# A fused attention and maxout kernel: the key and value projection of five batches moves into a down-layer bank at the first group spot

## The chip, the cores and the metric

The kernel runs on one core of a Trainium2 chip, as one program with one launch. The metric is the device time of one execution in microseconds (us). TensorE (PE) multiplies matrices and writes to PSUM; VectorE (DVE) and ScalarE (ACT) copy, add and evaluate functions; GpSimd (POOL) and SyncE (SP) issue the transfers here. Each engine works through its own instructions in the order in which the program gives them.

## The reference: what is computed

```
k_proj = einsum('ks,bhsd->bhkd', E, k);  v_proj = einsum('ks,bhsd->bhkd', F, v)
attn   = softmax(q @ k_proj^T / sqrt(64))          # over 64 projected keys
x      = (attn @ v_proj), heads side by side        # 8192 tokens x 512
out    = maximum(x @ w1, x @ w2) @ w_out            # 512 -> 1024 -> 512
```

There are 8 batches with 8 heads, 1024 positions and head size 64. Inputs and output are float32; the kernel multiplies in fp16.

## The kernel before

**Up and down layer.** With wd = w1 - w2 and m = w2 @ w_out, the output is relu(x @ wd) @ w_out + x @ m. From the second half-batch on, both matrix products are done as 2x2 block products with 7 block multiplications in place of 8. This needs sums of blocks of x (`sums_x`), of the relu'd activations (`sums_g`) and of the weights, all on VectorE (line 519).

**Units.** The 16 units are (batch, half of the positions), n = 0 to 15. While unit n does its down layer, unit n+1's up layer runs between. The down layer of a unit has 7 products (p1, p2, p6, p5, p7, p3, p4, line 636), each cut in three pieces of 4 matmuls in units 1 to 14. I write Pa.b for piece b of the a-th of them, from P0.0 to P6.2. The up layer of a unit has 14 products of 4 matmuls (line 558): seven, U0 to U6, after each of two group spots G0 and G1. A group spot does one step of attention for a later batch: the scores of a new group of heads (line 266), and the row sums and attention values of the group before (line 278).

**The order** is written out by hand in a list of slots; `at_slot` hangs steps behind a slot. For odd and even units n > 1 it is, with h = 0 first:

```
P0.0 P0.1 G0 P0.2 P1.0 | U0 P1.1 U1 P1.2 U2 P2.0 U3 P2.1 U4 P2.2 U5 P3.0 U6
P3.1 P3.2 G1 P4.0 P4.1 P4.2 | U0 P5.0 U1 P5.1 U2 ... U5 P6.2 U6
```

Unit 1 has three pieces ahead of G0 and three behind, and in its second half two ahead of G1 and one behind.

**PSUM.** There are four banks mm0 to mm3 and two pairs of banks "att". The down layer owns mm0 and mm1: products p1, p6, p7 and p4 build up in one (X), p2, p5 and p3 in the other (Y); X is mm0 in even units and mm1 in odd ones. The up layer and the scores use mm2 and mm3, sums and values the att pairs.

**What empties the banks.** ACT: the exponentials of the scores (line 355, two per spot), the logarithm of the sums (374), its inversion (377), copies of up and down products that are used twice (529), the last down product (704). DVE: the additions of the up layer (573, relu in 576), of the down layer (660), and the scaling of the attention values (381). In the up layer U0 and U2 build up in one bank, so U2 waits for the copy (529) of U0.

**Projection of k and v** (`step_kv`, line 180): 16 matmuls, 8 pairs of k and v side by side, for one batch. For batches 3 to 7 it hangs behind U1 of the first half of unit n = 2b-3 (units 3, 5, 7, 9, 11), in an att bank. Behind it come an ACT copy of k (line 191), and, one slot later, on DVE a copy of v (196), a second copy of k (198) and of v (200); then SP issues the transposing transfer of k (223), POOL waits for its landing (229) and issues the loads of the next batch (102). At G0 of the same unit SP has issued two transposing transfers of q (249). The new batch's first scores come at G1 of that unit. Batch 2 has its projection in unit 1, also in an att bank and behind U1, and this stays.

**Block sums for unit 2.** For the up layer of unit 2, which runs in unit 1, the sum S(2) = X(0,0) - X(1,0) hangs behind P1.2 of unit 1, and it is what U4 multiplies:

```
elif n == 2:
    where = (("P", 1, 0, 2), 0), (("P", 1, 1, 0), 1), (("P", 1, 1, 2), 2), (("U", 1, 0, 1), 3)
```

Later units have their sums behind slots of the second half of unit n-2. Steps behind a slot stand in the order in which they were hung there; behind P1.2 these are the addition of P1 (line 660), one sum of g and then S(2).

**The last unit** (15) has no up layer beside it; its seven products run in one piece each, and the last (p4) is emptied in two halves (line 699).

Of the kernel before, what the change touches and what calls it, by code (L numbers as in the profile page):

```python
# [16 lines left out]
def kernel(  # L17
# [42 lines left out]
    def mm_bank(dtype=FP32, n=None):  # L60
        if n is None:
            n = turn.pop(0)
            turn.append(n)
        return ps.tile([128, 512 if dtype == FP32 else 1024], dtype, tag=f"mm{n}", name="mm_ps")

    def att_banks(dtype=FP32):
        return ps.tile(
            [128, 2, 512 if dtype == FP32 else 1024], dtype, tag="att", bufs=2, name="att_ps"
        )
# [99 lines left out]
        t["qt"] = qtp.tile([128, H, HALF], FP16, tag="qt", name="qt_sb")  # L169


    def step_kv(t, h0=0, h1=H, which="kv", att=False, dma=False):
        kv_ps = att_banks()[:, 0, :] if att else mm_bank()
        n = (h1 - h0) * D
        both = which == "v"
        for c in range(NC):
            for w in which:
                i = "kv".index(w)
                for r in range(2) if both else (i,):
                    nc.tensor.matmul(  # L180
                        out=kv_ps[r * KP : (r + 1) * KP, 0:n],
                        lhsT=eft[:, i, c, :],
                        rhs=t[w][:, h0:h1, c, :],
                        start=(c == 0), stop=(c == NC - 1),
                    )
        fl = lambda ap: ap[:, h0:h1].rearrange("p h z d -> p (h z d)")
        zd = lambda ap: ap.rearrange("p (h d z) -> p h z d", d=D // 2, z=2)
        if "k" in which:
            eng = nc.vector.tensor_copy if which == "k" else nc.scalar.copy
            kp = t["kp"][:, h0:h1]  # L190
            eng(out=kp[:, :, 0, :], in_=kv_ps[0:KP, 0:n].rearrange("p (h d) -> p h d", d=D))
        if both:
            nc.vector.tensor_copy(out=t["vp"][:, h0:h1], in_=zd(kv_ps[:, 0:n]))
        elif "v" in which:
            def finish_v():
                nc.vector.tensor_copy(out=t["vp"][KP:128, h0:h1], in_=zd(kv_ps[KP:128, 0:n]))
                if dma:
                    nc.vector.tensor_copy(out=kp[:, :, 1, :], in_=kp[:, :, 0, :])
                    step_kpt_dma(t)
                nc.vector.tensor_copy(out=fl(t["vp"][0:KP]), in_=fl(t["vp"][KP:128]))  # L200

            if att:
                return finish_v
            finish_v()
# [405 lines left out]
    def down_steps(u, alone):  # L610
        b, o = u["b"], u["o"]
        st = {}
        xbank, ybank = (0, 1) if u["n"] % 2 == 0 else (1, 0)

        def cat(g, x):
            return lambda n: g[:, n] if n < NG else x[:, n - NG]

        def product(k, name, n, lo=0, hi=2 * (NG + NX)):
            if n is not None and (lo == 0 or alone):
                st[name] = mm_bank(n=n)  # L620
            bank = st[name]
            A = lambda j, h: cat(g_blk(u, j, h), x_blk(u, j, h))
            S = lambda i: cat(s_g(i), s_x(i, u))
            Bb = lambda h, c: cat(
                wo_sb[:, h * NG : (h + 1) * NG, c * CH : (c + 1) * CH],
                m_sb[:, h * NX : (h + 1) * NX, c * CH : (c + 1) * CH],
            )
            T = lambda i: lambda n: T_sb[:, i, n, :]
            a, w_ = {
                1: lambda: (A(0, 0), Bb(0, 0)), 2: lambda: (A(0, 1), Bb(1, 0)),  # L630
                3: lambda: (S(3), Bb(1, 1)), 4: lambda: (A(1, 1), T(3)),
                5: lambda: (S(0), T(0)), 6: lambda: (S(1), T(1)), 7: lambda: (S(2), T(2)),
            }[k]()
            for m in range(lo, hi):
                i, c = divmod(m, NG + NX)
                nc.tensor.matmul(  # L636
                    out=bank[:, i * CH : (i + 1) * CH],
                    lhsT=a(c)[:, i * 128 : (i + 1) * 128],
                    rhs=w_(c),
                    start=(n is not None and m == (lo if alone else 0)),  # L640
                    stop=(c == NG + NX - 1), skip_group_check=True,
                )
            return bank

        two = lambda ap: ap.rearrange("q (i m) -> q i m", i=2)

        def o_tile():
            return opool.tile([128, 2, CH], FP32, tag="o", name="o_sb")

        def store(j, c, o_sb, i0=0, i1=2):  # L650
            nc.sync.dma_start(
                out=out.rearrange("(n p i o) m -> n o p i m", p=128, i=NI, o=2)[
                    b, j, :, 2 * o + i0 : 2 * o + i1, c * CH : (c + 1) * CH
                ],
                in_=o_sb[:, i0:i1],
            )

        def add(j, c, x, y):
            o_sb = o_tile()
            nc.vector.tensor_tensor(out=o_sb, in0=two(x), in1=two(y), op=ALU.add)  # L660
            store(j, c, o_sb)

        def keep_d(bank):
            return keep("pd", bank, *([nc.vector.tensor_copy] if u["n"] == 0 else []))

        size = 2 * (NG + NX) // (1 if alone else 2 if u["n"] == 0 else 3)

        def piece(k, name, n, m):
            product(k, name, n, m, m + size)

        def whole(k, name, n):
            return product(k, name, n, 2 * (NG + NX) - size)

        def p1():
            st["s1"] = keep_d(whole(1, "X", xbank))

        def p2():
            add(0, 0, whole(2, "Y", ybank), st["s1"])

        def p6():  # L680
            st["u1"] = keep_d(whole(6, "X", None))

        def p5():
            st["s5"] = keep_d(whole(5, "Z", ybank))

        def p7():
            st["u2"] = keep_d(whole(7, "X", None))

        def p3():
            add(0, 1, whole(3, "Z", None), st["u1"])  # L690
            add(1, 1, st["u2"], st["s5"])

        def p4():
            o_sb = o_tile()
            if alone:
                for i in range(2):
                    bank = product(4, ("C", i), 2 + i, 6 * i, 6 * i + 6)
                    part = slice(i * CH, (i + 1) * CH)
                    nc.vector.tensor_tensor(
                        out=o_sb[:, i], in0=bank[:, part], in1=st["u2"][:, part], op=ALU.add,  # L700
                    )
                    store(1, 0, o_sb, i, i + 1)
                return
            nc.scalar.copy(out=o_sb, in_=two(whole(4, "X", None)))
            store(1, 0, o_sb)

        steps_ = (
            (p1, 1, "X", xbank), (p2, 2, "Y", ybank), (p6, 6, "X", None), (p5, 5, "Z", ybank),
            (p7, 7, "X", None), (p3, 3, "Z", None), (p4, 4, "X", None),
        )  # L710
        return [
            (*(lambda a=a, m=m: piece(*a, m) for m in range(0, 2 * (NG + NX) - size, size)), f)
            for f, *a in steps_
        ]
# [67 lines left out]
    for n, key in enumerate(units):  # L782
        downs = down_steps(U[key], n == last)
        if n in (0, last):
            for p, pieces in enumerate(downs):
                slots += [(("P", n, p, i), x) for i, x in enumerate(pieces)]
            continue
        pieces = [(("P", n, p, i), x) for p, x in enumerate(downs) for i, x in enumerate(x)]
        ups = [*up_steps(U[units[n + 1]])]
        for h, (x, y) in enumerate(((3, 3), (2, 1)) if n == 1 else ((2, 2), (2, 3))):  # L790
            slots += pieces[:x]
            slots.append((("G", n, h), lambda: None))
            slots += pieces[x : x + y]
            del pieces[: x + y]
            for i in range(7):
                slots.append((("U", n, h, i), ups.pop(0)))
                if i < 6:
                    slots.append(pieces.pop(0))
        assert not pieces and not ups
# [52 lines left out]
    for b in range(3, B):  # L852
        t = tiles[b]
        n = 2 * b - 3
        at_slot(("G", n, 0), new_attn, t)
        at_slot(("G", n, 0), step_qt_dma, t, 0, H // 2)
        at_slot(("G", n, 0), step_qt_dma, t, H // 2, H)
        at_slot(("U", n, 0, 1), step_kv, t, 0, H, "kv", True, True)
        at_slot(("U", n, 0, 6), step_gate, t)
        at_slot(("U", n, 0, 6), loads, b + 1, "k", "v", "q")  # L860
    groups = [(tiles[b], g, j) for b in range(1, B) for j in range(2) for g in range(2)][2:]
# [67 lines left out]
```

## Time and profile before

| | |
|---|---|
| five runs, median (lowest, highest) | 329.0 us (328.65, 330.51) |
| the profiled execution, its own time | 328.65 us |
| its span from first to last instruction | 326.9 us |
| copies at line 529 | 172, 593 ns each, 97.2 us |
| exponentials at line 355 | 50, 597 ns each |
| scaling at line 381 | 26, 1219 ns each |
| additions at line 660 (one input in PSUM) | 32, 685 ns each |
| output stores | 63 of 256 KB, 2.7 us to landing, and 2 of 128 KB |
| loads of v, of q | 17.3 and 22.0 us to landing |

The profile gives, for each engine, when an instruction started and how long it took, and in brackets how long the engine had been idle and what released it. Matmuls overlap: the modelled duration of one 128x256 matmul is 273 ns, but four of them in a row start 0.437 us before the next four. So on PE one reads the starts, and a delay is a distance between starts that is longer than it should be. The rows of the timeline merge neighbours of one kind ("x4").

### The profile page before, as it was taken

How to read it: one execution, taken by the hardware profiler on the slowest of the kernel's cores; microseconds unless marked ns; L12 is line 12 of the kernel's file. 1: busy time of each engine (PE TensorE's matmuls, PEld its weight loads, DVE VectorE, ACT ScalarE, POOL GpSimd, SP SyncE). 2: the span in 40 equal slices, each digit the busy share in tenths (PEclk: the TensorE clock that was granted, in tenths of full speed). 3: DMA queues.
4: the chain of work that ended last, by engine and by line, in shares of the span. 5: the costliest groups of instructions: out<-in, count | busy, mean ns of one | idle time of the engine just before them, and what ended most of it. 6: DMA issues, size and time to landing. Idle time of an engine off the chain costs nothing.

```text
span 326.9 us, 9015 instructions
## 1 busy us (share of the span) xinstructions
PE 317.4 (97%) x3856; PEld 248.6 (76%) x3856; DVE 239.5 (73%) x424; ACT 201.2 (62%) x359; POOL 36.9 (11%) x56
## 2 busy tenths in 40 slices
PE   8979999999999999999999999999999999999994
PEld 3544446877888788878887888878887888888883
DVE  1346798985969878677967796877967796969572
ACT  2465232666777577677776777657776777765541
POOL 8646002003000110003000300003000000000000
PEclk9999999999999999999999999999999999999999
DMA  8999999988999899996999599888999130212032
GB/s 157 205 198 176 207 207 208 218 189 156 184 239 232 125 154 237 195 194 96 213 221 183 109 183 244 194 162 122 226 191 213 43 99 32 98 34 98 33 130 96
DMA packets 74680, 53.14 MB, mean 163 GB/s; under 512 B 29456, under 2 KB 74512, under 8 KB 74640
## 3 DMA queue, kind: packets, MB, share of 16 engines
q0 software_dynamic: 29376, 28.31, 54.8%
q1 hardware_dynamic: 45264, 24.25, 31.0%
q8 instruction: 30, 0.49, 0.6%
q14 instruction: 10, 0.08, 0.1%
HBM read 57.15 MB, written 16.78 MB: 226 GB/s over the span
## 4 chain that ended last, share of the span: by engine, by line
PE 79%; DMA 14%; POOL 2%; DVE 2%; issue 1%; ACT 0%; DVEq 0%; POOLq 0%
PE mm_ps L636 43%; PE mm_ps L558 26%; DMA q_sb<-in_q_dram 8%; DMA v_sb<-in_v_dram 4%; PE att_ps L180 3%; PE att_ps L278 3%; PE mm_ps L266 3%; DMA big<-in_moe_w_dram 2%; POOL q_sb L102 1%; POOL k_sb L102 1%; DVE gt_sb L573 1%; PE mm_ps L237 1%; DVE o_sb L660 1%; POOL v_sb L102 0%; DVE xt_sb L381 0%
## 5 line engine op out<-in xcount | busy, mean ns | idle before, releaser
L529 ACT COPY p_sb<-mm_ps 128x512 f32<-128x512 f32 x172 | 97.2, 593 | 42.9 <-PE mm_ps L558 30.6
L636 PEld LDWEIGHTS <-big 128*128 128x128 f16 x768 | 73.6, 98 | 12.0 <-issue 3.5
L636 PE MATMUL mm_ps<-T_sb,big 128*128 128x256 f16 x576 | 77.9, 273 | 0.0
L573 DVE TENSOR_TENSOR gt_sb<-mm_ps,p_sb 128x512 f16<-128x512 f32 x56 | 38.5, 688 | 45.8 <-PE mm_ps L558 42.6
L558 PE MATMUL mm_ps<-big,big 128*128 128x256 f16 x336 | 50.4, 273 | 0.0
L558 PEld LDWEIGHTS <-big 128*128 128x128 f16 x448 | 43.8, 98 | 5.3 <-issue 0.2
L636 PEld LDWEIGHTS <-gt_sb 128*128 128x128 f16 x384 | 35.7, 98 | 9.7 <-issue 5.4
L636 PE MATMUL mm_ps<-wo_sb,gt_sb 128*128 128x256 f16 x256 | 42.9, 273 | 0.1
L558 PEld LDWEIGHTS <-wd_sb 128*128 128x128 f16 x336 | 32.9, 98 | 4.1 <-issue 0.4
L558 PE MATMUL mm_ps<-xt_sb,wd_sb 128*128 128x256 f16 x224 | 33.6, 273 | 0.2 <-ACT ex_sb L355 0.2
L355 ACT ACTIVATE ex_sb<-mm_ps 128x512 f16<-128x512 f32 x50 | 27.2, 597 | 9.6 <-PE att_ps L278 7.0
L381 DVE TENSOR_TENSOR xt_sb<-att_ps,ld_sb 128x1024 f16<-128x1024 f32 x26 | 31.7, 1219 | 0.1
L660 DVE TENSOR_TENSOR o_sb<-mm_ps,p_sb 128x512 f32<-128x512 f32 x32 | 21.9, 685 | 11.0 <-PE mm_ps L636 7.5
L636 PE MATMUL mm_ps<-m_sb,xt_sb 128*128 128x256 f16 x128 | 24.4, 273 | 0.0
L608 ACT ACTIVATE gt_sb<-mm_ps 128x512 f16<-128x512 f32 x28 | 16.8, 600 | 8.7 <-PE mm_ps L558 8.7
L519 DVE TENSOR_TENSOR big<-gt_sb 128x1024 f16<-128x1024 f16 x32 | 21.9, 684 | 0.2
L576 DVE TENSOR_SCALAR gt_sb<-gt_sb 128x512 f16<-128x512 f16 (+1 forms) x56 | 20.3, 363 | 1.9
L636 PE MATMUL mm_ps<-T_sb,gt_sb 128*128 128x256 f16 x128 | 21.5, 273 | 0.0
L636 PE MATMUL mm_ps<-wo_sb,big 128*128 128x256 f16 x128 | 21.5, 273 | 0.0
L636 PEld LDWEIGHTS <-xt_sb 128*128 128x128 f16 x192 | 18.8, 98 | 2.2
L229 POOL COPY junk<-kpt_sb 1x1 f16<-1x1 f16 x5 | 0.9, 178 | 162.1 <-DMA kpt_sb<-kp_sb 162.1
L573 DVE TENSOR_TENSOR gt_sb<-p_sb 128x512 f16<-128x512 f32 x28 | 19.1, 682 | 0.0
(85 smaller groups left out, 428.1 us busy)
## 6 DMA issues: line engine op xcount, KB each, us to landing
out_dram<-o_sb SPq DMA_DIRECT2D x63, 256.0 KB, 2.7
k_sb<-in_k_dram POOLq DMA_DIRECT2D x7, 1024.0 KB, 10.0
v_sb<-in_v_dram POOLq DMA_DIRECT2D x7, 1024.0 KB, 17.3
q_sb<-in_q_dram POOLq DMA_DIRECT2D x7, 1024.0 KB, 22.0
k_sb<-in_k_dram POOLq DMA_DIRECT2D x4, 256.0 KB, 6.4
q_sb<-in_q_dram POOLq DMA_DIRECT2D x4, 256.0 KB, 7.5
v_sb<-in_v_dram POOLq DMA_DIRECT2D x2, 512.0 KB, 12.5
big<-in_moe_w_dram POOLq DMA_DIRECT2D x8, 128.0 KB, 10.9
```

The costliest lines, as they stand in the source:

```text
L180: nc.tensor.matmul(out=kv_ps[r * KP : (r + 1) * KP, 0:n], lhsT=eft[:, i, c, :], rhs=t[w][:, h0:h1, c, :], start=(c == 0), stop=(c == NC - 1),)
L266: nc.tensor.matmul(out=banks[e][pos : pos + Z, h * W : (h + 1) * W], lhsT=t["kpt"][o * D : (o + 1) * D, head, s * Z : (s + 1) * Z], rhs=t[ ...
L355: nc.scalar.activation(out=t["ex", g, j][:, e, :], in_=banks[e], func=ACTF.Exp, scale=scale)
L381: nc.vector.tensor_tensor(out=x_out(t, g, j).rearrange("q z o n -> q o z n"), in0=at_ps.rearrange("q o (z n) -> q o z n", z=2), in1=ld[:, ...
L519: nc.vector.tensor_tensor(out=S(i), in0=x, in1=y, op=op)
L529: copy(out=x, in_=bank)
L558: nc.tensor.matmul(out=bank[:, m * W : (m + 1) * W], lhsT=w_[:, n_, (2 * d + m) * 128 : (2 * d + m + 1) * 128], rhs=a[:, n_, :], start=(n ...
L573: nc.vector.tensor_tensor(out=c_blk(j, c), in0=two(x), in1=two(y), op=ALU.add)
L576: nc.vector.tensor_scalar_max(ap, ap, 0.0)
L608: nc.scalar.activation(out=out, in_=in_, func=ACTF.Relu)
L636: nc.tensor.matmul(out=bank[:, i * CH : (i + 1) * CH], lhsT=a(c)[:, i * 128 : (i + 1) * 128], rhs=w_(c), start=(n is not None and m == (lo ...
L660: nc.vector.tensor_tensor(out=o_sb, in0=two(x), in1=two(y), op=ALU.add)
```

## The change

In units 3, 5, 7, 9 and 11 the projection moves from behind U1 to G0, ahead of the scores, and from an att bank to mm0, which is Y of these units. Its ACT and DVE copies follow at once, ahead of the exponentials of G0. In all odd units one piece (P1.0) moves from ahead of U0 to behind it, and so on through the first half, so that P3.0 stands behind U6. In unit 1 this makes two pieces ahead of G0 and one behind, and three ahead of G1 and three behind. The order in odd units is now

```
P0.0 P0.1 [kv in 3, 5, 7, 9, 11] G0 P0.2 | U0 P1.0 U1 P1.1 U2 P1.2 U3 P2.0 U4 P2.1 U5 P2.2 U6
P3.0 P3.1 P3.2 G1 P4.0 P4.1 P4.2 | U0 P5.0 U1 P5.1 ... P6.2 U6
```

In the last unit the addition of p7 and p5 runs right behind p7 instead of behind p3. The slots behind which the block sums hang have the same names as before. The number of instructions does not change.

```diff
-    def step_kv(t, h0=0, h1=H, which="kv", att=False, dma=False):
-        kv_ps = att_banks()[:, 0, :] if att else mm_bank()
+    def step_kv(t, h0=0, h1=H, which="kv", att=False, dma=False, n=None):
+        kv_ps = att_banks()[:, 0, :] if att else mm_bank(n=n)
...
         def p7():
             st["u2"] = keep_d(whole(7, "X", None))
+            if alone:
+                add(1, 1, st["u2"], st["s5"])

         def p3():
             add(0, 1, whole(3, "Z", None), st["u1"])
-            add(1, 1, st["u2"], st["s5"])
+            if not alone:
+                add(1, 1, st["u2"], st["s5"])
...
-        for h, (x, y) in enumerate(((3, 3), (2, 1)) if n == 1 else ((2, 2), (2, 3))):
+        for h, (x, y) in enumerate(((2, 1), (3, 3)) if n % 2 else ((2, 2), (2, 3))):
             slots += pieces[:x]
             slots.append((("G", n, h), lambda: None))
             slots += pieces[x : x + y]
...
         at_slot(("G", n, 0), step_qt_dma, t, H // 2, H)
-        at_slot(("U", n, 0, 1), step_kv, t, 0, H, "kv", True, True)
+        at_slot(("G", n, 0), step_kv, t, 0, H, "kv", False, True, 0)
         at_slot(("U", n, 0, 6), step_gate, t)
```

The rest of the diff renames a local variable.

## The prediction

> **What bounds the kernel now.** I read the page first: span, busy time by engine, the row of the granted clock.
>
> ```profile
> span 326.9 us, 9015 instructions
> ...
> PE 317.4 (97%) x3856; PEld 248.6 (76%) x3856; DVE 239.5 (73%) x424; ACT 201.2 (62%) x359; POOL 36.9 (11%) x56
> ...
> PEclk9999999999999999999999999999999999999999
> ```
>
> PE is the bound, at full clock, so what counts is where PE starts late. Next the timeline around the first half of unit 5 (batch 4), for what the moved step costs today.
>
> ```profile
> 138.49 0.41 PE L266 MATMUL mm_ps<-qt_sb,kpt_sb 64*32 64x256 f16 x16
> ...
> 138.96 1.08 ACT L355 ACTIVATE ex_sb<-mm_ps 128x512 f16<-128x512 f32 x2 [0.59 <-PE att_ps L278]
> ...
> 139.16 0.39 PE L636 MATMUL mm_ps<-wo_sb,gt_sb 128*128 128x256 f16 x2
> ...
> 141.45 0.40 PE L180 MATMUL att_ps<-k_sb,eft 128*64 128x512 f16 x1
> ...
> 143.30 0.39 PE L636 MATMUL mm_ps<-wo_sb,gt_sb 128*128 128x256 f16 x2
> 143.44 0.58 ACT L191 CAST kp_sb<-att_ps 64x512 f16<-64x512 f32 x1 [1.41 <-PE att_ps L180]
> ...
> 143.75 0.60 PE L558 MATMUL mm_ps<-big,big 128*128 128x256 f16 x4
> ...
> 148.46 0.68 DVE L573 TENSOR_TENSOR gt_sb<-mm_ps,p_sb 128x512 f16<-128x512 f32 x1
> ...
> 148.65 0.30 PE L278 MATMUL att_ps<-ex_sb,ones 64*32 64x256 f16 x8
> ...
> 149.54 0.72 PE L636 MATMUL mm_ps<-T_sb,big 128*128 128x256 f16 x5
> ```
>
> The spot G0 takes 0.67 us (138.49 to 139.16), kv 1.85 (141.45 to 143.30), and no row of this half waits for a bank. But G1 takes 0.89 (148.65 to 149.54): 0.22 more. Its scores wait for the DVE addition that frees mm3 (148.46 + 0.68 = 149.14), late because v's copies stand ahead of it.
>
> Third, the end of unit 1's first half on DVE and PE, and its second half, which already has one piece between spot and U0, as the odd units will have.
>
> ```profile
> 65.44 1.28 DVE L329 TENSOR_TENSOR xt_sb<-att_ps,ld_sb 128x512 f16<-128x512 f32 x2
> ...
> 66.78 0.41 PE L278 MATMUL att_ps<-ex_sb,vp_sb 64*32 64x256 f16 x16
> ...
> 69.96 0.42 DVE L519 TENSOR_TENSOR big<-xt_sb 128x512 f16<-128x512 f16 x1
> ...
> 72.44 0.69 DVE L196 CAST vp_sb<-att_ps 64x512 f16<-64x512 f32 x1 [0.80 <-ACT kp_sb L191]
> ...
> 73.89 0.60 PE L558 MATMUL mm_ps<-big,big 128*128 128x256 f16 x4
> ```
> ```profile
> 78.33 1.08 ACT L355 ACTIVATE ex_sb<-mm_ps 128x512 f16<-128x512 f32 x2 [0.93 <-PE mm_ps L266]
> ...
> 78.97 0.60 PE L558 MATMUL mm_ps<-xt_sb,wd_sb 128*128 128x256 f16 x4 [0.18 <-ACT ex_sb L355]
> ...
> 80.92 0.60 PE L558 MATMUL mm_ps<-big,big 128*128 128x256 f16 x4
> ```
>
> 69.96 is S(2), long done when U4 (73.89) reads it. The second fence gives the price of a short cover: U0 starts 0.64 after the exponentials do and U2 2.59 after; PE's own pace (0.437 a piece) would have had them 0.34 and a further 0.20 sooner.
>
> **Step 1, the five kv spots.** Count from the first kv matmul, 138.49 in unit 5. It needs mm0, free since 137.88 (line 704: 137.29 + 0.59), cover 0.6; and v's load, issued at 114.08 and landing 17.3 later, at 131.4, cover 7. ACT's cast starts 1.99 after kv starts (143.44 - 141.45); ACT starts one queued instruction 0.48 after the last (exponentials at 138.96, logarithm at 139.93), so the exponentials, now behind the cast, start at 2.47, though the scores are there by some 2.3 (1.75 to 1.85, plus 0.47). Then U0 at 2.47 + 0.64 = 3.11 and U2 at 2.47 + 2.59 = 5.06. Today U2 stands at 143.75 - 138.49 = 5.26 with one more piece done: 4.82 for equal work. Loss 0.24. P1.0 needs mm0 empty: v's copy can start when the cast ends (2.60; DVE's queue ends at 2.61) and ends at 3.30; P1.0's turn is 3.55, cover 0.25. Behind that copy DVE holds lines 198, 200 and U1's addition, which waits until 5.0 for U0's copy anyway and is done at 5.7; U3, which needs its bank, comes at 5.94. At G1 the addition that frees mm3 now ends by 9.2, and G1 comes at 10.4: the 0.22 go, and nothing is late next. Per spot +0.24 - 0.22 = +0.02, five times **+0.1**.
>
> How kv and scores follow each other directly the trace does not show. A change of matmul shape costs 0.09 in front (U1's start at 140.92 + 0.437 = 141.36, kv at 141.45); between kv and scores it is 0 to 0.14 (kv's eight pairs need 1.71 of its 1.85). Either way ACT is the later one, so I take 0.1 and lose nothing by it. "TensorEngine Tiling (Array Packing)", Key Properties, in the Trainium skill says that a change of tiling mode drains the array; by it the merged block saves one change in four, not two, which is the dearer end of that range.
>
> SP: the transfer of k stands behind both of q, which hold SP to 144.29 (138.45 + 5.84); it goes there and not at 145.75, and POOL's loads some 1.5 sooner. The store of P1's addition goes behind it, 1.2 later, into four buffers. PE waits for none of these; if loads collided, v's cover of 7 is what would be used up.
>
> **Step 2, unit 1, first half.** (a) G0 comes one piece sooner, but its value matmuls need an att pair that DVE empties until 65.44 + 1.28 = 66.72, and start at 66.78 as before. So the spot ends at 67.12 in both, with P0.2 still to do: +0.44. (b) P0.2, U0, P1.0, U1 bring kv to 67.12 + 4 x 0.437 + 0.09 = 68.96. S(2) hangs behind P1.2, which now follows kv, so in DVE's queue it moves behind v's copies, the scaling and the addition of P1. Cast 68.96 + 1.99 = 70.95 to 71.53, v's copy 71.56; then, by distances between starts in this half, line 200 +0.73, scaling +0.30, addition +1.14, sum of g +0.60, S(2) +0.60: 74.93 to 75.35. U4 can start at 75.40 (0.05 is what 66.72 to 66.78 shows). PE would be there at 68.96 + 1.85 + 5 x 0.437 = 72.99. Stall **2.41**. Nothing hides it: PE is in order, and U4 is its next instruction. (c) Second half: three pieces ahead of U0 instead of one, so 0.34 + 0.20 = 0.54 go. Sum +0.44 + 2.41 - 0.54 = **+2.3**. Bounds: S(2) not late at all, -0.1; half the queue again (1.7), +4.
>
> The Trainium skill, "PSUM — Partial Sum Buffer", PSUM bank collisions raise a hardware error, says that different quadrants of one bank may be read at once without harm. Cast and copy read different ones, so by this rule v's copy need not wait. The row says that it does here (idle 0.80, released by line 191, 0.03 after its end); without that wait the stall would be 0.6 shorter, and the sum +1.7.
>
> **Step 3, unit 13** (no kv, one piece behind G0): U0 at 0.67 + 0.44 = 1.11 and exponentials + 0.64 = 1.11: nothing. U2's turn is 1.11 + 1.75 = 2.86; the copy allows 0.47 + 2.59 = 3.06: **+0.2**.
>
> **Step 4, the end.**
>
> ```profile
> 321.90 0.68 DVE L660 TENSOR_TENSOR o_sb<-p_sb 128x512 f32<-128x512 f32 x1
> ```
>
> This goes to 320.6, where DVE idles. Before it SP issued four stores from 322.01 on, the last at about 323.6, 0.5 apart; one of them now goes early. Bounds: at least 0.2 (the last half of p4 is ready 0.36 after its last matmul's start at 322.24, as p3's was, and DVE reached it only at 322.84), at most the 0.6 between two of these issues; I take **-0.5**.
>
> **Sum.** 0.1 + 2.3 + 0.2 - 0.5 = +2.1 on the profiled execution's 328.65 (span 326.9, the rest around it unchanged): 330.7. That execution is 0.35 under the median 329.0, from which the sum is 331.1; I say **330.9**.
>
> **Rivals.** (R1) Not slower: S(2) is not late. Place: U4 of unit 1; price 2.4; it decides if S(2) starts by 72.5. For: S(2) needs only x, ready at 66.7. Against: DVE is in order, and the copy of v ahead of it cannot start before 71.5. 330.9 - 2.4 = 328.5. (R2) ACT keeps up at the kv spots: each gains 0.22 and two changes of shape (0.09 each) instead of +0.02, five times -0.42: 328.8. Against: the cast is ahead of the exponentials, and 2.47 is 0.2 late. (R3) The thin covers at the kv spots (0.25 for P1.0, 0.2 for U3) fail, 0.3 each time: 332.4. R1 with R2: 326.4.
>
> **Numbers.** Forecast 0.57, R1 0.10, R2 0.15, R3 0.13, R1 with R2 0.05. The range 328.6 to 332.5 takes in R2 and R3 and leaves R1 and the double case out. Within 0.5% of 329.0 (327.4 to 330.6, about what a measurement can tell from no change) lie R1, R2 and about 0.1 of the forecast: 0.35; faster is the double case, 0.05; slower 0.60.
>
> **What would show it.** In unit 1's first half PE idles about 2.4 just ahead of line 558's U4, released by DVE line 519, and no longer at 78.97. In units 3 to 11 U2 starts 2.6 after the exponentials, these right behind line 191, and G1 takes 0.67. SP's last burst has three stores. I am wrong if U4 follows P2.0 directly, or if P1.0 waits for line 196.

## The result, and the profile after

The median after is 331.05 us (329.71 to 333.94, 23 runs), beside 328.9 before (44 runs): the ratio is 1.0067 [1.005, 1.0085], slower. The forecast was 330.9.

To find the terms of the sum I cut each profiled execution in three on PE: up to the start of the 601st matmul (the prologue, ahead of all that the change touches), from there to the last matmul's start (the **body**), and from there to the end (the **tail**).

| us | before | after | difference | predicted |
|---|---|---|---|---|
| prologue | 61.09 | 60.26 | -0.83 | 0 |
| body | 261.15 | 263.56 | +2.41 | +2.6 (0.1 + 2.3 + 0.2) |
| tail | 4.65 | 3.93 | -0.72 | -0.5 |
| span | 326.9 | 327.8 | +0.9 | +2.1 |

The prologue's instructions are the same in both, and it took 59.9 to 60.4 in four of the kernels below (versions 1, 2, 3 and 5), which leave it alone too and kept full clock there: 61.09 is scatter of one execution, so spans are not compared here, bodies and tails are. They make +1.7. The medians differ by 2.15; they hold the granted clock of TensorE too, which is told below.

The page of after:

```profile
span 327.8 us, 9011 instructions
...
PE 317.4 (97%) x3856; PEld 249.0 (76%) x3856; DVE 239.8 (73%) x424; ACT 200.6 (61%) x359; POOL 37.9 (12%) x56
...
L558 PE MATMUL mm_ps<-big,big 128*128 128x256 f16 x336 | 50.4, 272 | 2.3 <-DVE big L519 2.2
```

PE's busy time is the same 317.4 to the digit: nothing was added to its work. (The four instructions fewer, 9011 for 9015, are semaphore instructions of ACT; each engine's work has the same count.) The new thing is the last column of the up products' group: 2.3 us of idle time, of which 2.2 ended with a block sum on DVE. Before, the same row had none:

```profile
L558 PE MATMUL mm_ps<-big,big 128*128 128x256 f16 x336 | 50.4, 273 | 0.0
```

The timeline of after around unit 1 shows where:

```profile
65.95 0.41 PE L278 MATMUL att_ps<-ex_sb,vp_sb 64*32 64x256 f16 x16 [0.26 <-DVE xt_sb L329]
...
70.74 0.69 DVE L196 CAST vp_sb<-att_ps 64x512 f16<-64x512 f32 x1 [1.07 <-ACT kp_sb L191]
...
71.75 0.60 PE L636 MATMUL mm_ps<-T_sb,big 128*128 128x256 f16 x4
...
73.51 0.68 DVE L519 TENSOR_TENSOR big<-gt_sb 128x1024 f16<-128x1024 f16 x1
74.11 0.42 DVE L519 TENSOR_TENSOR big<-xt_sb 128x512 f16<-128x512 f16 x1
...
74.59 0.61 PE L558 MATMUL mm_ps<-big,big 128*128 128x256 f16 x4 [2.23 <-DVE big L519]
...
79.33 1.48 PE L636 MATMUL mm_ps<-T_sb,big 128*128 128x256 f16 x12
80.65 0.60 PE L558 MATMUL mm_ps<-xt_sb,wd_sb 128*128 128x256 f16 x4
```

Read from the bottom of the stall upwards: U4 (74.59) starts 0.06 after S(2) ends (74.11 + 0.42); S(2) stands behind a sum of g and all that DVE did from v's copy at 70.74 on. PE's last piece started at 71.75, so U4's turn was 72.19: 2.40 lost. Below it, the second half's U0 follows three pieces without a wait. The first line is the other loss of unit 1: the value matmuls of G0 need the att pair that DVE empties. In before they came just as it was empty; now they come one piece sooner and wait.

The first half of unit 5 in after, with the projection in its new place:

```profile
139.96 0.40 PE L180 MATMUL mm_ps<-k_sb,eft 128*64 128x512 f16 x1
...
141.81 0.41 PE L266 MATMUL mm_ps<-qt_sb,kpt_sb 64*32 64x256 f16 x16
141.95 0.58 ACT L191 CAST kp_sb<-mm_ps 64x512 f16<-64x512 f32 x1 [2.10 <-PE mm_ps L180]
...
142.43 1.07 ACT L355 ACTIVATE ex_sb<-mm_ps 128x512 f16<-128x512 f32 x2
...
143.07 0.60 PE L558 MATMUL mm_ps<-xt_sb,wd_sb 128*128 128x256 f16 x4
...
144.99 0.60 PE L558 MATMUL mm_ps<-big,big 128*128 128x256 f16 x4
...
150.32 0.30 PE L278 MATMUL att_ps<-ex_sb,ones 64*32 64x256 f16 x8
...
151.00 1.27 PE L636 MATMUL mm_ps<-T_sb,big 128*128 128x256 f16 x10
```

From the first line on: cast at 1.99 (predicted 1.99), exponentials at 2.47 (2.47), U0 at 3.11 (3.11), U2 at 5.03 (5.06). G1 took 0.68 (150.32 to 151.00), 0.89 before. The end on DVE:

```profile
322.13 0.69 DVE L660 TENSOR_TENSOR o_sb<-p_sb 128x512 f32<-128x512 f32 x1 [2.72 <-ACT p_sb L529]
322.82 0.69 DVE L660 TENSOR_TENSOR o_sb<-mm_ps,p_sb 128x512 f32<-128x512 f32 x1
```

The addition that moved is the first of them: it now runs in an idle stretch of DVE, ahead of p3's. SP's last burst of stores, before and after:

```profile
322.01 2.00 SPq L651 DMA_DIRECT2D out_dram<-o_sb  x4
```
```profile
322.85 2.10 SPq L651 DMA_DIRECT2D out_dram<-o_sb  x4
```

### The profile page after: what moved, and what is told of

The parts are those of the page before. It is cut to its first block, busy times and chain, and to the rows that moved or that the text cites. A ratio compares the mean times of both kernels' runs of the same rounds, so it can differ in the third digit from the quotient of the medians.

```text
span 327.8 us, 9011 instructions
## 1 busy us (share of the span) xinstructions
PE 317.4 (97%) x3856; PEld 249.0 (76%) x3856; DVE 239.8 (73%) x424; ACT 200.6 (61%) x359; POOL 37.9 (12%) x56
## 4 chain that ended last, share of the span: by engine, by line
PE 85%; DVE 6%; DMA 5%; POOL 2%; issue 1%; ACT 0%; DVEq 0%; POOLq 0%
PE mm_ps L636 43%; PE mm_ps L558 26%; DMA v_sb<-in_v_dram 4%; PE mm_ps L404 4%; PE att_ps L278 3%; PE mm_ps L180 3%; PE mm_ps L266 2%; PE mm_ps L440 2%; DMA big<-in_moe_w_dram 1%; DVE xt_sb L329 1%; PE att_ps L180 1%; POOL q_sb L102 1%; POOL k_sb L102 1%; DVE o_sb L660 1%; DVE xt_sb L381 1%
## 5 line engine op out<-in xcount | busy, mean ns | idle before, releaser
L636 PE MATMUL mm_ps<-T_sb,big 128*128 128x256 f16 x576 | 76.5, 273 | 0.0
L576 DVE TENSOR_SCALAR gt_sb<-gt_sb 128x512 f16<-128x512 f16 (+1 forms) x56 | 21.3, 380 | 1.9
L229 POOL COPY junk<-kpt_sb 1x1 f16<-1x1 f16 x5 | 1.8, 357 | 163.1 <-DMA kpt_sb<-kp_sb 163.1
```

Of the source, the lines that this page charges most:

```text
L576: nc.vector.tensor_scalar_max(ap, ap, 0.0)
L636: nc.tensor.matmul(out=bank[:, i * CH : (i + 1) * CH], lhsT=a(c)[:, i * 128 : (i + 1) * 128], rhs=w_(c), start=(n is not None and m == (lo ...
```

## The experiments

**Theory.** The whole loss is one thing: in unit 1, S(2) comes late on DVE, since the slot it hangs behind now follows the projection. The rest of the change is near zero: the kv spots +0.02 each, the tail a gain. **Rivals.** The loss comes from unit 1's own reordering or the kv spots (each had thin covers), and the idle time is only where it shows. And of the clock: that it falls by chance and not because of the idle time.

**1. S(2) sooner.** After, with one key changed, two pieces sooner:

```diff
-            where = (("P", 1, 0, 2), 0), (("P", 1, 1, 0), 1), (("P", 1, 1, 2), 2), (("U", 1, 0, 1), 3)
+            where = (("P", 1, 0, 2), 0), (("P", 1, 1, 0), 1), (("P", 1, 1, 0), 2), (("U", 1, 0, 1), 3)
```

> The changed kernel with one edit: in unit 1 the block sum S(2) hangs behind P1.0 (with S(1)) instead of behind P1.2. Theory (S(2)'s place in DVE's queue makes U4 late): the 2.40 us idle time of PE ahead of U4 in unit 1 is gone, U4 follows P2.0 after 0.44, and nothing else changes; the time falls by 2.4 us from 331.05 to about 328.6, a ratio to the kernel before of 0.999. Rival (U4 waits for its bank or its weights, and DVE's line 519 only happened to come last): U4 still waits, more than 1 us, and the time stays above 330. Second rival (the clock: part of the slower time is a lower granted clock after the idle time, since executions of the changed kernel show 0.992 to 0.995 more often than not): with the idle time gone the clock is 1.00 in all runs and the time falls by more than 2.4, to 328 or less.

Measured 327.84, ratio to before 0.9961 [0.9943, 0.9979]; body 261.14, tail 3.90. Its timeline in unit 1:

```profile
68.04 0.42 DVE L519 TENSOR_TENSOR big<-xt_sb 128x512 f16<-128x512 f16 x1
...
72.30 0.60 PE L558 MATMUL mm_ps<-big,big 128*128 128x256 f16 x4
```

S(2) runs at 68.04, ahead of v's copies, and U4 follows at its turn. One subtraction in another place of DVE's queue takes back the whole body loss (263.56 to 261.14, 2.42). The medians differ by 3.2, more than 2.4, and 327.84 is what the second rival, the clock, had forecast, though not with a full clock in every execution (two of 12 list 0.994 and 0.995). Among the executions with a mean clock of 0.9965 or more the medians are 330.01 and 327.72, which is 2.3 apart: queue and clock both count.

**2. Unit 1 as before, all else as after.**

```diff
-        for h, (x, y) in enumerate(((2, 1), (3, 3)) if n % 2 else ((2, 2), (2, 3))):
+        for h, (x, y) in enumerate(((3, 3), (2, 1)) if n == 1 else ((2, 1), (3, 3)) if n % 2 else ((2, 2), (2, 3))):
```

> The changed kernel, but unit 1 keeps its old order of three and three, two and one pieces. Theory (unit 1 is the whole loss): 0.1 for the kv spots, 0.2 for unit 13, -0.5 to -0.6 for the end, sum -0.2 to -0.3, so 328.6 to 328.7, ratio 0.999, and the half-microsecond waits ahead of U0 and U2 in unit 1's second half are back. Rival (the kv spots gain, and unit 1 hid it): below 328, ratio under 0.997.

Measured 327.72, 0.9967 [0.9948, 0.9987]; body 261.25, which is 0.10 over before's: unit 13's 0.2, and -0.1 for the five kv spots together. Unit 1's old waits of 0.34 and 0.20 are back. By its time alone the rival (a gain at the kv spots) would have won: 327.72 is under its 328 and the ratio under its 0.997. The trace does not bear it out: with -0.02 a spot the kv spots are worth next to nothing. The tail gave 0.1 to 0.2 more than expected and the body 0.2 more; the rest of the difference is the one that stays open below.

**3. Unit 1's new order alone, on before.**

```diff
-        for h, (x, y) in enumerate(((3, 3), (2, 1)) if n == 1 else ((2, 2), (2, 3))):
+        for h, (x, y) in enumerate(((2, 1), (3, 3)) if n == 1 else ((2, 2), (2, 3))):
```

> The kernel before with the new order of pieces in unit 1 alone. Theory: +0.44 +2.41 -0.54 = +2.3 in the body, 331.2, ratio 1.007, and the same 2.4 us idle time ahead of U4. Rival (the loss needs the moved kv too): ratio below 1.003. The clock: if the idle time itself lets the granted clock fall, this kernel shows it below 0.996 in about as many executions as the changed one.

Measured 331.85, 1.0097 [1.0062, 1.0132]: the loss is there without the moved projection. It is 0.8 over the whole change, whose tail is 0.7 shorter, but the intervals of the two ratios overlap. Its body is 265.0, +3.85, though unit 1's order was to cost 2.3. The windows of this execution show the other 1.55 (window, length, then busy us and count of PE, PEld, DVE, ACT, POOL, granted clock, DMA share, GB/s):

```profile
72.00:74.90 2.90, 0.67 (x7) 0.35 (x6) 2.69 (x4) 0.59 (x1) 0.00 (x0) 1.00 1.09 203
74.90:78.30 3.40, 3.40 (x31) 2.25 (x30) 0.57 (x2) 0.59 (x1) 0.26 (x2) 0.50 0.95 213
78.30:80.00 1.70, 1.70 (x17) 1.53 (x16) 1.67 (x3) 1.09 (x2) 1.70 (x3) 1.00 0.20 8
```

In the first window PE stands still for 2.23 us, waiting for S(2). In the second it is busy without a gap, but at half the granted clock; in the third the clock is back. 3.41 us at half speed can lose up to 1.7 (an estimate; the body shows 1.55). After's own profiled execution is one in which this did not happen. Of its 24 executions, this one among them, 15 list a lower mean clock (below 0.9965; one such stretch takes 0.005 off the mean), and these have a median of 332.03, the other nine 330.01.

**4. A version without the move:** before, with the last unit's edit as in the change; unit 1 with three pieces ahead of G0 and two behind, and one ahead of G1 and three behind; and the fourth sum of g one piece later, out of the way of the addition that G1 waits for.

```diff
-        for h, (x, y) in enumerate(((3, 3), (2, 1)) if n == 1 else ((2, 2), (2, 3))):
+        for h, (x, y) in enumerate(((3, 2), (1, 3)) if n == 1 else ((2, 2), (2, 3))):
...
-            for key, i in (end, 0), (("P", n, 0, 0), 1), (("P", n, 1, m), 2), (("P", n, 2, m), 3):
+            for key, i in (end, 0), (("P", n, 0, 0), 1), (("P", n, 1, m), 2), (("P", n, 3, 0) if m else ("P", n, 2, m), 3):
```

> The kernel before with three edits that the reading suggests: the addition of the last unit sooner (as in the change), in unit 1 three pieces ahead of G0 and two behind, one ahead of G1 and three behind, and the last sum of g (S(3)) hung behind P3.0 instead of P2.2, so that the addition which frees mm3 for the scores of G1 stands ahead of it on DVE. Theory: -0.5 at the end, -0.54 in unit 1, -0.22 at each G1 of units 3 to 11, sum -2.1, so 326.8, ratio 0.9935. Rival for the last one (G1's 0.22 is a change of matmul shape, not DVE): the spots keep 0.89 and the ratio is 0.997.

Measured 326.56 (326.07 to 327.15), 0.9935 [0.9914, 0.9956]: faster than before and after, as expected (326.8). Body 259.52, -1.63: 0.54 from unit 1's second half and 0.22 at each of five G1, which is 1.64. G1 of unit 5 in this kernel:

```profile
147.67 0.68 DVE L573 TENSOR_TENSOR gt_sb<-mm_ps,p_sb 128x512 f16<-128x512 f32 x1
...
148.45 0.30 PE L278 MATMUL att_ps<-ex_sb,ones 64*32 64x256 f16 x8
...
149.12 1.48 PE L636 MATMUL mm_ps<-T_sb,big 128*128 128x256 f16 x12
```

The addition ends at 148.35, ahead of G1, which takes 0.67. So the gain at G1 is to be had without moving the projection; all that the move has besides is one spared change of matmul shape, about 0.1 a spot.

**5 and 6. How long must PE stand still for the clock to fall?** In 5, S(2) hangs one slot sooner than in after, where it should cost 1.2; in 6 two repeats of another block sum (same inputs, same result, extra work) stand ahead of it on DVE.

```diff
-            where = (("P", 1, 0, 2), 0), (("P", 1, 1, 0), 1), (("P", 1, 1, 2), 2), (("U", 1, 0, 1), 3)
+            where = (("P", 1, 0, 2), 0), (("P", 1, 1, 0), 1), (("U", 1, 0, 2), 2), (("U", 1, 0, 1), 3)
```

> The changed kernel with S(2) of unit 1 hung behind U2, so that in DVE's queue it stands behind the scaling, but ahead of the addition of P1 and the sum of g (0.60 each). Theory of the queue: the idle time of PE ahead of U4 is 2.40 - 1.20 = 1.20 us. Theory of the clock (an idle time of 2.4 us now and then lets the granted clock fall to half for 3.4 us, which costs some 1.6 more; a shorter one does not): clock 1.00 ahead of the end in all executions, and the time is that of the kernel without the idle time (327.84) + 1.2 = 329.0, 2.0 under the changed kernel. Rival (any idle time lowers the clock about in proportion, or the wide spread of the changed kernel has another cause): clock 0.992 to 0.995 in a third of the executions or more, and 329.8 or above.

```diff
+    for _ in range(2):
+        at_slot(("P", 1, 1, 2), sums_g, U[0, 1], (2,))
```

> The changed kernel with the sum of g ahead of S(2) in unit 1 done three times instead of once (it writes the same values again), so that S(2) is 1.2 us later still. Theory of the queue: PE idles 3.6 us ahead of U4. Theory of the clock: now nearly every execution has a stretch of 3.4 us at half clock behind it (clock near 0.995), so the time is 327.84 + 3.6 + 1.6 = 333.0. Rival (idle time costs only itself): clock as in the changed kernel, 331.05 + 1.2 = 332.2 or less.

Version 5: 328.97 (expected 329.0), 0.9997 [0.9981, 1.0013]; body 262.35; the clock is 0.998 or more in all 12 executions. Version 6: 334.67 (expected 333.0), 1.0146 [1.0121, 1.0171]; the clock fell in all 6 (0.983 to 0.995). U4 in 5 and in 6, and the window behind it in 6:

```profile
73.52 0.61 PE L558 MATMUL mm_ps<-big,big 128*128 128x256 f16 x4 [1.03 <-DVE big L519]
```
```profile
77.45 1.03 PE L558 MATMUL mm_ps<-big,big 128*128 128x256 f16 x4 [3.69 <-DVE big L519]
```
```profile
77.00:83.80 6.80, 6.35 (x43) 4.40 (x44) 3.14 (x7) 1.77 (x3) 2.82 (x4) 0.50 0.72 123
```

The distances say 1.19 and 3.84 of delay. In 6 the half clock lasts 6.8 us, twice the stretch of version 3, and this execution has a stretch in the prologue as well. I had priced one stretch: the two executions with a mean clock of 0.994 and 0.995 took 332.9, as expected, the other four (0.983 to 0.988) 334.4 to 335.3. The number of drops grows with the length of the idle time (0 of 12, 15 of 24, 6 of 6, beside 15 of 94 in the kernels without it), so chance alone is out.

**7. Version 4 with the projection moved as in the change** (units 3, 5, 7, 9 and 11 alone, with `step_kv` as in the change).

```diff
-        for h, (x, y) in enumerate(((3, 2), (1, 3)) if n == 1 else ((2, 2), (2, 3))):
+        for h, (x, y) in enumerate(((3, 2), (1, 3)) if n == 1 else ((2, 1), (3, 3)) if n in (3, 5, 7, 9, 11) else ((2, 2), (2, 3))):
...
-        at_slot(("U", n, 0, 1), step_kv, t, 0, H, "kv", True, True)
+        at_slot(("G", n, 0), step_kv, t, 0, H, "kv", False, True, 0)
```

> The three edits of the earlier kernel (326.56) and on top of them the moved kv: in units 3, 5, 7, 9, 11 kv at G0 in mm0, two pieces ahead and one behind. Theory (the move's gain is only the 0.22 at G1, which the sum of g hung later gives without it; its loss of 0.14 at U0 and 0.18 at U2, less one change of matmul shape, 0.1, stays): +0.2 per spot, +1.0 to +1.1 in the body, 327.6, ratio to the kernel before 0.9965. Rival (the move gains by itself, by the spared change of shape and bank): 326.5 or less, ratio 0.993.

Measured 327.51, 0.9932 [0.9916, 0.9948]. The time is the theory's and the ratio is the rival's (the two medians, 327.51 and 328.96, would give 0.9956), and beside version 4 the intervals of the ratios overlap; so the traces decide: body 260.62 against 259.52, +1.10, or 0.22 a spot. PE waits 0.14 ahead of U0 and 0.18 ahead of U2 in unit 5, 0.3 in all at each of the five spots, less the change of shape that is saved.

**8. The cast of k on DVE.** Version 1 with the cast of line 191 taken from ACT, so that the exponentials are not behind it.

```diff
-            eng = nc.vector.tensor_copy if which == "k" else nc.scalar.copy
+            eng = nc.vector.tensor_copy if which == "k" or n == 0 else nc.scalar.copy
```

> The changed kernel with S(2) sooner (327.84, no long idle time), and the cast of k at the five kv spots on DVE instead of ACT. Theory (at these spots ACT's cast ahead of the exponentials is what makes U0 and U2 late, and mm0's cover is only 0.25): the exponentials start right behind the scores, 2.3 after kv, and U0 is not late any more; but DVE does cast and copy one after the other from 2.6, 0.7 each, so mm0 is free at 4.05 and P1.0, whose turn is 3.4, waits 0.6 to 0.7: +0.3 per spot, 329.4, ratio to the kernel before 1.001. Rival (mm0 has more cover than thought): P1.0 does not wait, five times -0.3, 326.4.

Measured 328.7, 0.9992 [0.9974, 1.0009], 0.7 under the expected time; body 262.5, +1.36 over version 1, 0.27 a spot, which is the theory's +0.3. The spot of unit 5:

```profile
141.77 0.60 PE L558 MATMUL mm_ps<-xt_sb,wd_sb 128*128 128x256 f16 x4
142.04 0.69 DVE L196 CAST vp_sb<-mm_ps 64x512 f16<-64x512 f32 x1
...
142.78 0.60 PE L636 MATMUL mm_ps<-wo_sb,gt_sb 128*128 128x256 f16 x4 [0.41 <-DVE vp_sb L196]
```

U0 is in time now (0.45 behind the piece ahead of it, at 141.32), so the cast ahead of the exponentials was what held it. But v's copy now starts 3.24 after the first projection matmul (138.80), 2.65 in after, and P1.0, which needs its bank, waits 0.57 instead (142.78 against a turn at 141.77 + 0.437). The wait moved, and grew.

## Why the prediction was right, and where it was off

| step | predicted | measured | by |
|---|---|---|---|
| 1, five kv spots | +0.1 | -0.1 | body of version 2, less unit 13 |
| 2a, G0 of unit 1 | +0.44 | 0.43 wait | after, value matmuls at 65.95 |
| 2b, S(2) late | +2.41 | 2.40; gone with S(2) alone | after; version 1 (2.42) |
| 2c, second half | -0.54 | -0.54 | waits back in version 2 |
| 3, unit 13 | +0.2 | 0.19 | after |
| 4, the end | -0.5 | -0.72 to -0.75 | tails 4.65, 4.66 without and 3.90 to 3.93 with the edit |
| the clock | none | 2.0 in over half of the executions | after, medians 332.03 and 330.01; versions 3, 5, 6 |

**Step 1 held.** ACT was the later one at every spot, by about 0.3 (0.14 at U0 and 0.18 at U2 in unit 5). The unknown in it, how scores follow the projection directly, measured 0.10: the scores come 0.31 after the last pair, pairs 0.21 apart. As the step said, it cost nothing, since ACT was later still. P1.0 never waited for line 196, the sign that would have refuted it; version 8 shows how near it was.

**Step 2 held to 0.01** in its largest term, since all of it came from distances that the trace of before had. That is what version 1 confirms by taking it away, and version 3 by having nothing else. Rival R1 is out by the same run: S(2) was late, and only because of its place. R2 is out by the spot's timeline (the exponentials start at 2.47, behind the cast), R3 too: no cover failed. DVE waited for ACT's cast again (70.74, released by line 191), and the stall was the longer of the two that the prediction had, 2.4 and not 1.8. A kernel without that wait was not tried, as the wait alone would have had to be taken away; so the rule of the Trainium skill, "PSUM — Partial Sum Buffer", PSUM bank collisions raise a hardware error, on reading different quadrants at once is neither borne out nor refuted here: the row shows a wait, not what two reads at once would do.

**Step 4 was mis-sized.** I took 0.5 between bounds of 0.2 and 0.6, and it gave 0.72 to 0.75, past the upper bound. I had counted on three stores in the last burst. There are still four. In before the burst began at 322.01, 0.23 ahead of the last matmul's start (61.09 + 261.15 = 322.24), in after at 322.85, 0.97 ahead of it (323.82): all of it is 0.74 earlier against PE. DVE, too, starts the very last half 0.31 after that matmul's start (324.13), before 0.60 (322.84). Which of the two sets the end was not separated.

**What was missing is the clock.** No step priced what a 2.4 us hole does to PE afterwards. That the forecast of 330.9 came within 0.15 of the median is in part luck: the traces make +1.7 of the parts it did have (2.4 - 0.7) where it had +2.1, and the executions of after that kept their clock have a median of 330.01, 0.3% over before and inside what a measurement can tell from no change. That the median lies beyond 0.5% is due to the clock. One difference stays open: +1.1 in these nine executions is less than the traces' +1.7, and the medians of versions 1, 2, 5 and 8 too lie 0.3 to 0.9 below their traces' sums, while those of 4 and 7 agree within 0.2. Before's trace is a single execution, and how typical its body is was not measured.

## What to carry to other kernels

When work is moved in a hand-written order, list for every slot that changes its place what hangs behind it on other engines, and walk that engine's queue from the new place to the first reader: a 0.4 us subtraction with its input ready 8 us before cost 2.4 us of an otherwise full TensorE. Then ask of the gain which queue it really comes from; here the 0.22 at G1 was to be had by moving one sum on DVE, without the projection. And a single hole of some 2 us in TensorE's stream is priced with the clock behind it.

## What the runs showed of the hardware

The granted clock can fall to 0.50 after a hole in PE's stream, for 3.41 us at a time, and the hole need not be that long:

| PE's delay | executions with a mean clock below 0.9965 | half clock in the profile |
|---|---|---|
| none there (before) | 4 of 23 and 3 of 23 | none |
| none there (versions 1, 2, 4, 7, 8) | 2 of 12, 2 of 12, 2 of 6, 1 of 6, 1 of 12 | in the prologue (4, 7, 8) |
| 1.19 (version 5) | 0 of 12 | none |
| 2.40 (after) | 15 of 24 | none in the profiled one |
| 2.39 (version 3) | 3 of 6 | 3.4 us |
| 3.84 (version 6) | 6 of 6 | 6.8 us, and 3.4 in the prologue |

The few in kernels without a hole have another place, as far as they were profiled: in versions 4, 7 and 8 the clock falls in the prologue, some 8 us after the start. Some of after's 15 may be of that kind. The Trainium skill, "TensorE: Matmul & The Clock Gate", What's actually happening, gives a free-running window of 3413 ns, of which one idle one brings half clock. The stretches of 3.41 and 6.8 us agree with one and two such windows. That a whole window must be idle does not agree: no 2.4 us hole holds one, and it was enough in half of the executions or more, though not in all.

The traces tell more, since the clock's changes in one profile lie whole windows apart: in version 3 it rises at 6.63 and falls at 74.90, which is 20 times 3.413. Counted from there, each profile's windows can be laid beside PE's idle time:

| window of | from and to | PE idle in it | share of the window | the clock behind it |
|---|---|---|---|---|
| after, the hole | 70.59 to 74.00 | 1.65 | 0.48 | full |
| version 3, the end | 324.07 to 327.49 | 1.80 | 0.53 | full |
| version 5, the end | 321.69 to 325.10 | 2.08 | 0.61 | half |
| version 3, the hole | 71.49 to 74.90 | 2.23 | 0.65 | half |
| version 6, the hole | 73.59 to 77.00 | 3.23 | 0.95 | half |

So where in the windows a hole falls decides: in after the boundary at 74.00 cut it in two, in version 3 one window held all of it. In the ten profiles, after the first 9 us, every window at full clock that was idle for 0.53 or less kept it, and every one idle for 0.61 or more was followed by half clock; between the two nothing was measured, and PE's idle time is itself only as good as the modelled ends of matmuls. The second stretch of version 6 followed a window at half clock with 0.45 us idle (77.00 to 80.41), and the clock came back after one without idle time. The drops in the prologue fit none of this: there PE was idle for 0.21 of the window at most, and why the clock fell stays open.
